# Five instructions fewer in VectorE's stream: two angle tables and pairs of column differences made in shared operations

## Chip, cores, metric

One Trainium2 chip, one core. The metric is the device time of one execution in microseconds (us). Of one execution in each job there is a profile; the span is the time from the first to the last instruction in it. Time and span differ by about 2 us, called the *time outside the span* below.

## The reference, cut

```python
xn = layernorm(x)                                   # x: [1, 2048, 512]
# A: a diagonal complex recurrence over 2048 steps
Bu = einsum("bld,pd->blp", xn + 0j, B_bar)
h_t = Lam_bar * h_{t-1} + Bu_t                      # 2048 steps, 512 complex states
yA = 2 * einsum("blp,dp->bld", hseq, C).real + xn * Dskip
# B: a gated product
yB = einsum("bsf,fd->bsd", silu(xn @ w1) * (xn @ w3), w2)   # 512 -> 1792 -> 512
out = x + yA + yB
```

The kernel works in four blocks of 512 tokens. The recurrence is turned into real scans on VectorE by rotating each state with a table of cosines and sines ("angle tables", one for each of four groups of 128 states). Part of the matrix products is done by a scheme with seven products instead of eight, which needs sums and differences of quarters of both operands (s1 to s4 of the weights, t1 to t4 of the activations, the "column differences").

## The kernel before: what the change touches

The angle table of a group is four VectorE operations, then two sines on ScalarE that are queued:

```python
def table_angles(pt):
    if pt >= 3:
        sin_step((pt - 3, 0))
    ang, rnd = slot32[pt], slot32[NPT + pt]
    nc.vector.tensor_scalar(out=ang, in0=iota_f, scalar1=turn[:, pt:pt + 1], scalar2=None, op0=ALU.mult)
    nc.vector.tensor_scalar(out=rnd, in0=ang, scalar1=MAGIC, scalar2=None, op0=ALU.add)
    nc.vector.scalar_tensor_tensor(out=ang, in0=rnd, scalar=MAGIC, in1=ang, op0=ALU.subtract, op1=ALU.subtract)
    nc.vector.tensor_scalar(out=rnd.bitcast(DT.int32), in0=ang.bitcast(DT.int32), scalar1=0x7FFFFFFF, ...)
    ...                                             # two sines appended to `sins`
```

The column differences are made for block 2 (in `bu_sums`, mixed with the weights' sums) and for block 3 (in `column_list`):

```python
((t1, b12, b11), (t2, b22, t1), (t3, b22, b12), (t4, b21, t2))   # out, x, z: out = x - z, 128x512 each
```

t1 and t3 subtract neighbours of the same kind (b12 - b11 and b22 - b12), so one operation over a wider view can make both. Small work for VectorE is queued with an estimated cost and filled in between larger steps, so a changed cost can move instructions:

```python
bg.add(1.9, lambda: table_angles(2))
bg.add(1.9, lambda: table_angles(3))
```

The first matmuls need x, normalised by VectorE, and the first columns of w1 and w3:

```python
load_w(0, 2 * P); load_w(2 * P, 4 * P)              # w1, then w3, 256 columns each time
keep_busy(NWARM, TBLK)                              # idle matmuls while nothing has landed
...
def quarter(cl, fs, parts=1):                       # chunk cl of 128 tokens
    for side, w in ((0, w1_sb), (1, w3_sb)):
        ...                                         # matmuls of 128 columns
quarter(0, (0, 1), 2)
quarter(1, (0, 1))
pps = params_transpose()                            # a tiny matmul, a useful mark in the trace
```

## Time and profile before

| | kernel before |
|---|---|
| time, median of 3 runs | 201.6 us (201.19 to 202.13) |
| profiled run: time, span | 201.48 us, 199.3 us |
| TensorE busy, VectorE busy | 195.4 us, 182.6 us |
| VectorE instructions, counted as busy / in the built program | 262 / 314 |

A busy share near 100% on TensorE says little by itself, because the ends of matmuls are modelled.

### The profile page before, as it was taken

To read this page: it belongs to the slowest core of one execution; us is meant where nothing else is said; L and a number is where in the kernel's file an instruction comes from. 1 tells how busy PE (TensorE), PEld (TensorE's weight loads), DVE (VectorE), ACT (ScalarE), POOL (GpSimd) and SP (SyncE) were. 2 spreads that over 40 slices of the span, in tenths; PEclk is the share of its full clock that TensorE was granted. 3 is DMA by queue.
4 is the path that set the end of the run, shared out by engine and by line. 5 is a ranking of instruction groups with operands and counts; after the bars stand their busy time and mean duration, and the time that the engine had idled before them with its cause. 6 is when DMAs were issued, how large, how long until landed. Compare 5 with 4: busy or idle time off the path is not lost.

```text
span 199.3 us, 3709 instructions
## 1 busy us (share of the span) xinstructions
PE 195.4 (98%) x1401; PEld 130.6 (66%) x1401; DVE 182.6 (92%) x262; ACT 134.9 (68%) x281; POOL 51.3 (26%) x75
## 2 busy tenths in 40 slices
PE   8999999999999999999999999999999999999994
PEld 2774444444444488866555478888566678888893
DVE  3699799999999999989999997999999999999972
ACT  4799897699999996968997684362588782111220
POOL 7170379800411135041202305040021303310000
PEclk9999999999999999999999999999999999999999
DMA  6999998990398054830997455838147732941111
GB/s 152 319 268 224 304 174 157 326 268 1 57 181 153 0 98 83 135 112 0 156 150 118 91 92 100 176 77 130 53 60 129 149 55 54 173 92 36 53 44 40
DMA packets 32258, 25.12 MB, mean 126 GB/s; under 512 B 16240, under 2 KB 29936, under 8 KB 32240
## 3 DMA queue, kind: packets, MB, share of 16 engines
q0 software_dynamic: 6128, 11.38, 33.6%
q1 hardware_dynamic: 25536, 13.21, 27.4%
q10 hardware_dynamic: 576, 0.30, 0.7%
q8 instruction: 11, 0.18, 0.4%
q14 instruction: 7, 0.06, 0.1%
HBM read 7.74 MB, written 2.10 MB: 49 GB/s over the span
## 4 chain that ended last, share of the span: by engine, by line
PE 95%; DMA 2%; SPq 1%; issue 0%; DVE 0%
PE gu_ps L583 34%; PE gu_ps L1043 17%; PE y_ps L1043 10%; PE gu_ps L837 7%; PE bu_ps L1043 7%; PE y_ps L450 3%; PE bu_ps L450 3%; PE y_ps L858 3%; PE y_ps L769 3%; DMA w_sb<-in_B_w_dram 2%; PE gu_ps L615 2%; PE gu_ps L769 2%; PE bu_ps L858 1%; PE bu_ps L769 1%; PE bu_ps L615 1%; SPq L166 0%
## 5 line engine op out<-in xcount | busy, mean ns | idle before, releaser
L583 PE MATMUL gu_ps<-xnT,w_sb 128*128 128x512 bf16 x312 | 69.6, 379 | 0.0
L583 PEld LDWEIGHTS <-w_sb 128*128 128x128 bf16 x312 | 30.5, 98 | 34.2
L1043 PEld LDWEIGHTS <-act 128*128 128x128 f16 x462 | 43.5, 98 | 5.4
L592 ACT ACTIVATE g<-gu_ps 128x512 bf16<-128x512 f32 x41 | 24.8, 606 | 5.9 <-PE gu_ps L583 3.1
L593 ACT ACTIVATE u<-gu_ps 128x512 bf16<-128x512 f32 x41 | 24.8, 606 | 4.4 <-PE gu_ps L583 4.1
L501 DVE TENSOR_TENSOR_SCAN u<-rho,ends,u 128x512 bf16<-128x512 f32 x16 | 20.0, 1271 | 0.0
L523 POOL DMA_DIRECT2D act<-p x7 | 9.2, 1321 | 33.9 <-DVE act L515 21.9
L1043 PE MATMUL gu_ps<-w_sb,act 128*128 128x256 bf16 (+3 forms) x126 | 15.9, 267 | 0.0
L837 PE MATMUL gu_ps<-xnT,w_sb 128*128 128x512 bf16 x64 | 15.9, 379 | 0.0
L600 DVE TENSOR_TENSOR act<-g,u 128x1024 f16<-128x1024 bf16 x21 | 14.2, 679 | 0.0
L849 ACT ACTIVATE g<-gu_ps 128x512 bf16<-128x512 f32 x14 | 8.4, 599 | 5.4 <-PE gu_ps L837 5.0
L450 PEld LDWEIGHTS <-bt 128*128 128x128 bf16 x64 | 6.3, 98 | 7.6
L1066 ACT ACTIVATE x_blk<-gu_ps 128x256 f32<-128x256 f32 (+1 forms) x9 | 3.3, 368 | 10.6 <-PE gu_ps L1043 10.6
L1043 PE MATMUL bu_ps<-w_sb,act 128*128 128x256 bf16 (+3 forms) x84 | 10.4, 264 | 0.0
L1043 PE MATMUL gu_ps<-ct,act 128*128 128x256 f16 (+1 forms) x72 | 10.4, 267 | 0.0
L837 PEld LDWEIGHTS <-w_sb 128*128 128x128 bf16 x64 | 6.2, 98 | 4.8
L501 DVE TENSOR_TENSOR_SCAN u<-rho,u 128x512 bf16<-128x512 f32 x8 | 9.2, 1207 | 0.0
L1043 PEld LDWEIGHTS <-x_blk 128*128 128x128 f16 x88 | 8.6, 98 | 1.0
L1043 PEld LDWEIGHTS <-tw 128*128 128x128 f16 x88 | 8.6, 98 | 1.0
L509 DVE TENSOR_TENSOR p<-u,tabe 128x2048 f16<-128x2048 bf16 (+1 forms) x8 | 8.7, 1085 | 0.0
L515 DVE TENSOR_TENSOR act<-u,tabe 128x2048 f16<-128x2048 bf16 (+1 forms) x8 | 8.7, 1085 | 0.0
L484 DVE TENSOR_TENSOR u<-u,tabe 128x2048 bf16<-128x2048 bf16 x7 | 8.5, 1220 | 0.1
(203 smaller groups left out, 393.9 us busy)
## 6 DMA issues: line engine op xcount, KB each, us to landing
act<-p POOLq DMA_DIRECT2D x6, 512.0 KB, 6.1
xn<-x_blk POOLq DMA_DIRECT2D x4, 512.0 KB, 6.0
out_dram<-xn SPq DMA_DIRECT2D x15, 128.0 KB, 1.7
w_sb<-in_B_w_dram SPq DMA_DIRECT2D x1, 1792.0 KB, 8.2
act<-act POOLq DMA_DIRECT2D x5, 352.0 KB, 4.6
w_sb<-in_B_w_dram SPq DMA_DIRECT2D x2, 768.0 KB, 6.1
u<-p POOLq DMA_DIRECT2D x3, 512.0 KB, 5.6
w_sb<-in_B_w_dram SPq DMA_DIRECT2D x4, 256.0 KB, 4.6
```

The costliest lines, as they stand in the source:

```text
L450: nc.tensor.matmul(out=ps, lhsT=bt[:, ri, dt, pt * P:(pt + 1) * P], rhs=xnT_blk[b][:, dt, :], start=(dt == 0), stop=(dt == NDT - 1))
L501: nc.vector.tensor_tensor_scan(out=v, data0=rho[:, pt:pt + 1].to_broadcast([P, TBLK]), data1=v, initial=init, op0=ALU.mult, op1=ALU.add)
L509: nc.vector.tensor_tensor(out=by_state(st["p16"][:, csl]), in0=by_chunk(st["g"][:, :, ::-1, tsl]), in1=by_chunk(tabe[:, psl, 2:0:-1, tsl]) ...
L515: nc.vector.tensor_tensor(out=by_state(act_state(b, hf)[:, csl]), in0=by_chunk(st["g"][:, :, :, tsl]), in1=by_chunk(tabe[:, psl, 0:1, tsl] ...
L523: gp.dma_start(out=a, in_=p16, accum_op=ALU.add)
L583: nc.tensor.matmul(out=ps[:, tsl], lhsT=w[:, dt, f * P:(f + 1) * P], rhs=xnT[:, dt, tsl], start=(dt == 0), stop=(dt == NDT - 1))
L592: nc.scalar.activation(out=g16[:, f % 2, :], in_=g_ps, func=ACT.Silu)
L593: nc.scalar.activation(out=u16[:, f % 2, :], in_=u_ps, func=ACT.Copy)
L600: nc.vector.tensor_tensor(out=act_gates(b, f - 1), in0=split(g16), in1=split(u16), op=ALU.mult)
L769: nc.tensor.matmul(out=out[:, h * TH:(h + 1) * TH], lhsT=left[:, h, k, :], rhs=right[:, k, :], start=(start and h == 0 and k == 0), stop=( ...
L837: nc.tensor.matmul(out=ps, lhsT=w[:, dt, f * P:(f + 1) * P], rhs=xnT[:, dt, :], start=(dt == 0), stop=(dt == NDT - 1))
L1043: nc.tensor.matmul(out=out, lhsT=left[:, k, :], rhs=right[k][:, cols], start=(start and k == 0), stop=(k == NK - 1), skip_group_check=True)
```

## The change

Its intent is a shorter VectorE stream: each operation has a fixed part, and a wider one pays it once (in the trace before, 128x512 took 420 ns, 128x1024 690). Tables 2 and 3 share three of their four operations (8 instructions become 5), and t1 and t3 of blocks 2 and 3 are made together (4 become 3, twice). The estimated cost of the queued sums of block 2 also goes from 0.36 to 0.38. The core of the diff:

```diff
-    def table_angles(pt):
+    def table_angles(pt, n=1):
...
-        ang, rnd = slot32[pt], slot32[NPT + pt]
-        nc.vector.tensor_scalar(out=ang, in0=iota_f, scalar1=turn[:, pt:pt + 1], ...)
+        slots = scratch[:, ...].bitcast(FP32).rearrange("p (h i t) -> p h i t", h=2, t=TBLK)
+        ang, rnd = slots[:, 0, pt:pt + n, :], slots[:, 1, pt:pt + n, :]
+        for i in range(n):
+            nc.vector.tensor_scalar(out=ang[:, i, :], in0=iota_f, scalar1=turn[:, pt + i:pt + i + 1], ...)
         nc.vector.tensor_scalar(out=rnd, in0=ang, scalar1=MAGIC, ...)          # now 128x1024, as the next two
...
-                for out, x, z in ((t1, b12, b11), (t2, b22, t1), (t3, b22, b12), (t4, b21, t2))]
+                for out, x, z in column_steps(b, t, (t1, t2, t3, t4))]
+    def column_steps(b, t, parts):
+        both = xnT_blk[b].rearrange("p (i k) (j t) -> p i k j t", i=2, j=2)
+        return ((t[:, 0::2], both[:, :, :, 1, :], both[:, 0].rearrange("p k j t -> p j k t")), (t2, b22, t1), (t4, b21, t2))
...
-    bg.add(1.9, lambda: table_angles(2))
-    bg.add(1.9, lambda: table_angles(3))
+    bg.add(3.6, lambda: table_angles(2, 2))
```

More of the change, by code (lines that the diff above doesn't have):

```diff
@@ L367, in params_w @@
         gp.tensor_scalar(out=wrn, in0=wr, scalar1=-1.0, scalar2=None, op0=ALU.mult)
-    def table_angles(pt):
-        if pt >= 3:
-            sin_step((pt - 3, 0))
-        ang, rnd = slot32[pt], slot32[NPT + pt]
-        nc.vector.tensor_scalar(out=ang, in0=iota_f, scalar1=turn[:, pt:pt + 1], scalar2=None, op0=ALU.mult)
+    def table_angles(pt, n=1):
+        if pt + n > 3:
+            sin_step((pt + n - 4, 0))
+        slots = scratch[:, 0:2 * NPT * 2 * TBLK].bitcast(FP32).rearrange("p (h i t) -> p h i t", h=2, t=TBLK)
+        ang, rnd = slots[:, 0, pt:pt + n, :], slots[:, 1, pt:pt + n, :]
+        for i in range(n):
+            nc.vector.tensor_scalar(out=ang[:, i, :], in0=iota_f, scalar1=turn[:, pt + i:pt + i + 1], scalar2=None,
+                                    op0=ALU.mult)
         nc.vector.tensor_scalar(out=rnd, in0=ang, scalar1=MAGIC, scalar2=None, op0=ALU.add)
@@ L378, in table_angles @@
                                 op0=ALU.bitwise_and)
-        for i, (src, bias, scale) in enumerate(((rnd, halfpi, -TWO_PI), (ang, 0.0, -TWO_PI))):
-            sins.append(((pt, i), lambda i=i, src=src, bias=bias, scale=scale: nc.scalar.activation(
-                out=tabe[:, pt, i, :], in_=src, func=ACT.Sin, bias=bias, scale=scale)))
+        for k in range(pt, pt + n):
+            for i, (src, bias, scale) in enumerate(((rnd, halfpi, -TWO_PI), (ang, 0.0, -TWO_PI))):
+                sins.append(((k, i), lambda k=k, i=i, src=src[:, k - pt, :], bias=bias, scale=scale: nc.scalar.activation(
+                    out=tabe[:, k, i, :], in_=src, func=ACT.Sin, bias=bias, scale=scale)))
     def weight_c(pt):
@@ L717, in column_list @@
         return [lambda out=out, x=x, z=z: nc.vector.tensor_tensor(out=out, in0=x, in1=z, op=ALU.subtract)
-                for out, x, z in ((t1, b12, b11), (t2, b22, t1), (t3, b22, b12), (t4, b21, t2))]
+                for out, x, z in column_steps(b, t, (t1, t2, t3, t4))]
+    def column_steps(b, t, parts):
+        t1, t2, t3, t4 = parts
+        b11, b12, b21, b22 = quarters(b)
+        both = xnT_blk[b].rearrange("p (i k) (j t) -> p i k j t", i=2, j=2)
+        return ((t[:, 0::2], both[:, :, :, 1, :], both[:, 0].rearrange("p k j t -> p j k t")), (t2, b22, t1), (t4, b21, t2))
     def bu_quarter(hf, kh, r, half=False):
@@ L733, in bu_columns @@
     def bu_columns(b):
-        return ups["t"] if b == 3 else [v.rearrange("p (k a) t -> p k (a t)", k=2) for v in spare_slots(k_gate(10))]
+        if b == 3:
+            return ups["t"]
+        return act(2)[:, :, k_gate(10):k_gate(10) + 4, :].rearrange("p c (k a) t -> p c k (a t)", k=2)
     def bu_sums(b):
@@ L742, in bu_sums @@
                           (s4, a12, s2, ALU.subtract)])
-        t1, t2, t3, t4 = bu_columns(b)
-        b11, b12, b21, b22 = quarters(b)
-        cols = [(*v, ALU.subtract) for v in ((t1, b12, b11), (t2, b22, t1), (t3, b22, b12), (t4, b21, t2))]
-        first = [t for two in zip(tasks[0], cols) for t in two]
-        return [(0.36, lambda out=out, x=x, y=y, op=op: nc.vector.tensor_tensor(out=out, in0=x, in1=y, op=op), ("bu", hf))
+        t = bu_columns(b)
+        cols = [(*v, ALU.subtract) for v in column_steps(b, t, [t[:, i] for i in range(4)])]
+        first = [t for two in zip(tasks[0], cols) for t in two] + tasks[0][3:]
+        return [(0.38, lambda out=out, x=x, y=y, op=op: nc.vector.tensor_tensor(out=out, in0=x, in1=y, op=op), ("bu", hf))
                 for hf, part in ((0, first), (1, tasks[1])) for out, x, y, op in part]
@@ L752, in bu_fast @@
         s1, s2, s3, s4 = bu_rows(hf)
-        t1, t2, t3, t4 = bu_columns(b)
+        t = bu_columns(b)
+        t1, t2, t3, t4 = (t[i] if b == 3 else t[:, i] for i in range(4))
         b11, b12, b21, b22 = quarters(b)
```

## The prediction

> **What bounds the kernel now.** I read the page of the kernel before first, then the chain that ended last in order of time, then TensorE's own waits, then VectorE's groups with shapes kept apart, then the timeline around the places that the change touches.
>
> The page's first part:
>
> ```profile
> PE 195.4 (98%) x1401; PEld 130.6 (66%) x1401; DVE 182.6 (92%) x262; ACT 134.9 (68%) x281; POOL 51.3 (26%) x75
> ```
>
> TensorE (PE) shows 98%, VectorE (DVE) 92%. A busy share alone does not prove that TensorE is the limit, since the ends of matmuls are modelled. So I look at the pace of their starts, in the chain that ended last (start, length, what):
>
> ```profile
> 28.41 24.17 PE gu_ps L583 x112
> 78.25 8.41 PE gu_ps L1043 x77
> 162.92 7.21 PE gu_ps L1043 x66
> ```
>
> 24.17 us over 112 matmuls of 512 columns is 215.8 ns each; 8.41 over 77 and 7.21 over 66 of 256 columns are 109.2 ns each, both times. The pace is the same early, in the middle and late. I went through the starts of all 1401 matmuls in the trace: from 8.6 us to the last one at 196.6 us, the distances are these values (and 55 to 56 ns for 128 columns) nearly without exception; what lies above them adds up to less than 0.2 us, most of it in three steps near 146, 153 and 159 us, where a matmul follows an evacuation by ScalarE (ACT) that itself follows a matmul. TensorE's own waits confirm it; this is the whole list:
>
> ```profile
> PE bu_ps L196 <- PEq L1257: 0.8, 1, 0.8
> PE gu_ps L615 <- DMA w_sb<-in_B_w_dram: 0.4, 1, 0.4
> ```
>
> Both are in the first 7 us. VectorE is waited for by TensorE's matmuls nowhere (its weight loads wait 1.0 us for a normalised x at 5 us, in code that the change leaves alone). So the time is: about 8.6 us of start, 188 us of matmuls at full pace, 2.7 us from the last matmul to the end of the span, and some 2.2 us outside the span (201.5 us for the profiled run against a span of 199.3).
>
> **What the Trainium skill says.**
> - "Perfetto Trace Analysis", section "Identifying the Most-Contended Engine": matmul occupancy is not a good measure of how near to the roofline a kernel is. I therefore rest on start distances. "TensorE: Matmul & The Clock Gate", section "Wait — 56ns, not 53.3ns?", gives 215.7 ns start to start at 512 columns once warm, and 55.6 at 128; the trace agrees (215.8 and 55 to 56 ns). There is nothing left to gain between two matmuls.
> - "VectorE: DVE Perf Modes", section "The TRN2 errata — SBUF-src ops pay a fixed extra latency per instruction": one large tile pays a fixed cost once, many small ones pay it each time; the measured fixed term is about 150 cycles. The trace agrees: with bf16 operands, one `tensor_tensor` of 512, 1024 and 2048 elements takes 420, 690 and 1219 ns, so 270 ns for 512 elements more and about 150 ns fixed. This is what the change saves.
> - Same page, section "The DRAIN you can't avoid": the next operation does not start until the pipe is empty. Here the trace says something finer, and it decides: an independent successor of a 420 ns operation starts 340 ns after its start, so before its recorded end, while one that reads its result starts 450 ns after it. So the real saving per removed instruction is about 70 to 80 ns where instructions are independent, and a merge can cost something where it puts a reader right behind its writer.
>
> **The change part by part.** The order of the instructions of the two built programs is the same on TensorE (all 2804 rows but for line numbers), on GpSimd and SyncE, and on ScalarE apart from line numbers. VectorE loses five instructions and has a few neighbours swapped. VectorE's groups before that the sums use (count, busy us, mean ns, idle before):
>
> ```profile
> L376 DVE SCALAR_TENSOR_TENSOR tw<-tw 128x512 f32<-128x512 f32 x4 | 2.8, 697 | 0.1
> L374 DVE TENSOR_SCALAR tw<-tw,turn 128x512 f32<-128x512 f32 x4 | 1.9, 478 | 1.6 <-POOL turn L325 1.6
> L377 DVE TENSOR_SCALAR tw<-tw 128x512 int32<-128x512 int32 x4 | 1.8, 442 | 0.1
> L375 DVE TENSOR_SCALAR tw<-tw 128x512 f32<-128x512 f32 x4 | 1.7, 428 | 0.1
> L966 DVE TENSOR_TENSOR tw<-ct 128x1024 f16<-128x1024 f16 x2 | 1.4, 690 | 0.0
> L717 DVE TENSOR_TENSOR x_blk<-xnT 128x512 f16<-128x512 bf16 x2 | 0.8, 418 | 0.0
> ```
>
> (1) *Angle tables 2 and 3*: 8 instructions become 5. Before: 2 x (478+428+697+442) = 4.09 us busy, and 4.08 us from start (14.79 us) to the next instruction (18.87). After, estimated: the two multiplications by a column stay (0.96); the fp32 `tensor_scalar` of 512 costs like a bf16 `tensor_tensor`, so at 1024 elements it should be about 0.70 (twice); the `scalar_tensor_tensor` runs at one element per cycle, 697 + 533 = 1.23. Sum 3.58, saving 0.51 us busy and about 0.46 us of VectorE's time. The sines of tables 2 and 3 read the result: table 2 is ready at about 18.3 us instead of 16.9, but ScalarE starts the sine of table 2 only at 25.48. No wait.
>
> (2) *Column differences for block 2* (L747): 4 instructions of 0.42 become one of 1024 elements (0.69) and two of 0.42. Start to start: 4 x 0.335 = 1.34 before, 0.60 + 2 x 0.335 = 1.27 after: 0.07 us saved. The first reader on TensorE loads weights that go with t1 at 90.28 us, 1.02 us after t1 was written; t1 now comes 0.27 us later. It still fits.
>
> (3) *The same for block 3* (L717): before, 113.51 to 114.97 = 1.46 us. After, t2 follows at once on the merged operation that it reads (0.72), t4 on t2 (0.45), then 0.34: 1.51. This one gains nothing, and may lose 0.05 us.
>
> Sum: busy time 182.6 - 0.51 - 8x0.419 + 2x0.69 + 4x0.42 = about 181.8 us in 257 instructions. Of this, TensorE sees nothing. The 0.46 us of (1) moves VectorE forward from 18.4 us; the statistics that follow are also done before a gate product that used to stand in between (0.6 us), so GpSimd's reciprocal root comes about 1 us earlier, and VectorE's wait for it (1.24 us, ending 24.57) stays a wait, merely earlier. The scans begin about 0.45 us earlier. VectorE still ends up waiting for TensorE:
>
> ```profile
> 86.77 0.69 DVE L1128 TENSOR_TENSOR xn<-gu_ps,x_blk 128x512 bf16<-128x512 f32 x1 [0.56 <-PE gu_ps L1043]
> ```
>
> There any lead from the first part is given back to idle time. The saving is hidden twice over: TensorE did not wait for VectorE, and VectorE waits for TensorE later.
>
> **The rivals.**
> - *A new wait takes the place of the old order and stalls TensorE.* The weakest place I found is near 110 us. There the copy of the states' ends (L1204) now comes ahead of a gate product (L600) that ScalarE waits for:
>
> ```profile
> 110.50 0.68 DVE L600 TENSOR_TENSOR act<-g,u 128x1024 f16<-128x1024 bf16 x1
> ...
> 111.70 0.16 DVE L1204 COPY ends<-act 128x8 f16<-128x8 f16 x1
> ```
>
>   The copy needs a transfer (act<-p, L523) issued at 104.68 and landed at 110.07. Its margin was 1.63 us and becomes about 0.4. That transfer took 5.4 us; the seven of this line took 4.2 to 8.6. If it landed x later, L600 would be x - 0.4 late, and so would ScalarE's evacuation at 111.30, which the matmul at 113.33 follows with 1.43 us to spare. So TensorE stalls only if the transfer takes more than 5.4 + 0.4 + 1.43 = 7.2 us; with the worst seen, 8.6, the loss is 1.4 us (203.0). Elsewhere (the gate products moved by 1.1 us near 35 and 52 us, and from 22.7 to about 24 us) three buffers of g and u stand between the product and its next writer; I expect no wait there.
> - *VectorE is the real bound, at 92%.* Then the saving of about 0.5 us would come through as 201.1. For it: VectorE is idle for only some us of the steady part, and ScalarE waits for L600 by 1.5 us at 111.30. Against: that ScalarE wait is absorbed before 113.5 us, and TensorE's starts show no gap there.
> - *Transfers start earlier and collide.* VectorE's lead of up to half a microsecond between 26 and 85 us moves the accumulating transfers that follow it. The mean DMA load is 126 GB/s and their readers came long after them; I give it no time.
>
> **Range and chances.** TensorE's stream is unchanged and without gaps, so I expect the median of before, 201.6 us. The three runs of before lie between 201.2 and 202.1; allowing for that spread, for 0.2 us of luck and for a rare late transfer, 201.0 to 202.3. Faster by 2% would need 4 us out of a stream that has less than 0.2 us of gaps: 1%. Slower by 2% needs several late waits at once: 1.5%.
>
> **What would show it.** Right: TensorE's two waits as before and the same pace of 215.8 and 109.2 ns; VectorE at about 181.8 us in 257 instructions; three 1024-wide instructions near 16 us of about 0.70, 1.23 and 0.70; the wait for GpSimd's root still there, ending near 23.5 us; the three instructions of block 3 no quicker than the four. Wrong: a line in TensorE's waits that names ScalarE or VectorE, a start distance above the pace near 113 us, or L1204 with idle time before it that ends with a DMA; or a span below 199 us with the same pace, which would mean that time was lost where I saw none.

## The result, and the profile after

Ratios are the mean time of one kernel's fast runs over that of the other's of the same rounds, so not quite the ratio of the medians quoted beside them.

| | before | after |
|---|---|---|
| time, median of 6 runs | 201.57 us (201.18 to 202.13) | 200.81 us (200.68 to 201.28) |
| ratio | | 0.9968, 95% interval 0.9949 to 0.9988 |
| profiled run: time, span | 201.48, 199.3 us | 200.71, 198.9 us |

The changed kernel is 0.3% quicker, well within the 2% that counts as the same, but below the predicted range of 201.0 to 202.3 us.

The page of the kernel after, first part:

```profile
PE 195.2 (98%) x1401; PEld 130.7 (66%) x1401; DVE 182.2 (92%) x257; ACT 135.0 (68%) x281; POOL 50.9 (26%) x75
```

The chain that ended last, after (start, length, what; the three pieces that answer to those of before):

```profile
27.98 24.17 PE gu_ps L587 x112
77.83 8.41 PE gu_ps L1055 x77
162.49 7.21 PE gu_ps L1055 x66
```

The lengths are the same to the last digit. All that differs is where the pieces stand: 0.43, 0.42 and 0.43 us earlier. So TensorE's pace did not change, and what it gained in this run it had already gained by 28 us. The timeline of TensorE around 7 us shows where; its last line is the transpose of the parameters, the mark. First before, then after (start, length, operation, in brackets the idle time and what ended it):

```profile
6.11 0.61 PE L615 MATMUL gu_ps<-xnT,w_sb 128*128 128x128 bf16 x8
7.12 1.35 PE L615 MATMUL gu_ps<-xnT,w_sb 128*128 128x128 bf16 x21 [0.40 <-DMA w_sb<-in_B_w_dram]
...
8.56 0.18 PE L315 MATMUL y_ps<-ident,par_rows 12*128 12x12 bf16 x1
```

```profile
6.16 2.04 PE L619 MATMUL gu_ps<-xnT,w_sb 128*128 128x128 bf16 x32
8.14 0.18 PE L315 MATMUL y_ps<-ident,par_rows 12*128 12x12 bf16 x1
```

Before, the ninth of these matmuls waited for the first columns of w3, which landed at 7.07 us in this execution; after, they landed at 6.64. The first merged instruction stands at 15.30 us, eight microseconds later: no merged work comes early enough to have brought that load in. TensorE's waits after, the whole list:

```profile
PE bu_ps L196 <- PEq L1268: 0.8, 1, 0.8
PE y_ps L243 <- DVE xn L224: 0.2, 1, 0.2
```

So two of the prediction's own signs of being wrong came up: a line that names VectorE (0.2 us, for the first normalised x, in code that the change leaves alone), and a span below 199 us at the same pace. Both lie in the start.

The lengths of the merged instructions are as worked out. VectorE's groups by shape, after (count, busy us, mean ns, idle before):

```profile
L379 DVE SCALAR_TENSOR_TENSOR tw<-tw 128x1024 f32<-128x1024 f32 x1 | 1.2, 1224 | 0.0
L380 DVE TENSOR_SCALAR tw<-tw 128x1024 int32<-128x1024 int32 x1 | 0.7, 695 | 0.0
L378 DVE TENSOR_SCALAR tw<-tw 128x1024 f32<-128x1024 f32 x1 | 0.7, 694 | 0.0
L721 DVE TENSOR_TENSOR x_blk<-xnT 128x1024 f16<-128x1024 bf16 x1 | 0.7, 685 | 0.0
```

The stretch of tables 2 and 3 saved more than was worked out. Its first line and the line that follows it, before and then after:

```profile
14.79 0.48 DVE L374 TENSOR_SCALAR tw<-tw,turn 128x512 f32<-128x512 f32 x1
18.87 0.69 DVE L219 BATCH_NORM_STATS2 stats<-x_blk 128x6 f32<-128x512 bf16 x1
```

```profile
14.39 0.88 DVE L376 TENSOR_SCALAR tw<-tw,turn 128x512 f32<-128x512 f32 x2
17.90 0.69 DVE L219 BATCH_NORM_STATS2 stats<-x_blk 128x6 f32<-128x512 bf16 x1
```

From 4.08 us it fell to 3.51, so VectorE gained 0.57 us here and not 0.46: the two multiplications now stand side by side and together take 0.88 us in place of 0.96, which is most of the difference. None of it reached TensorE's pace.

And the tight place near 110 us. Block 3's first difference and the line that follows the four, before:

```profile
113.51 0.42 DVE L717 TENSOR_TENSOR x_blk<-xnT 128x512 f16<-128x512 bf16 x1
114.97 0.69 DVE L600 TENSOR_TENSOR act<-g,u 128x1024 f16<-128x1024 bf16 x1
```

VectorE's timeline there after:

```profile
110.01 0.17 DVE L1215 COPY ends<-act 128x8 f16<-128x8 f16 x1
110.08 0.69 DVE L604 TENSOR_TENSOR act<-g,u 128x1024 f16<-128x1024 bf16 x1
...
113.01 0.69 DVE L721 TENSOR_TENSOR x_blk<-xnT 128x1024 f16<-128x1024 bf16 x1
113.73 0.88 DVE L721 TENSOR_TENSOR x_blk<-xnT,x_blk 128x512 f16<-128x512 bf16 x2
114.53 0.68 DVE L604 TENSOR_TENSOR act<-g,u 128x1024 f16<-128x1024 bf16 x1
```

The copy of the ends shows no idle time: its transfer had landed at 109.58, 0.43 us ahead. Block 3's differences take 113.01 to 114.53 = 1.52 us, against 1.46 before.

There is a second piece. Time minus span is 2.18 us for the profiled run before and 1.81 after; over the six runs after it is 1.74 to 1.88. The prediction took this time as given.

### The profile page after: what moved, and what is told of

Read it like the earlier page. It is cut to its first block, busy times and chain, and to the rows that moved or that the text cites. A ratio compares the mean times of both kernels' runs of the same rounds, so it can differ in the third digit from the quotient of the medians.

```text
span 198.9 us, 3703 instructions
## 1 busy us (share of the span) xinstructions
PE 195.2 (98%) x1401; PEld 130.7 (66%) x1401; DVE 182.2 (92%) x257; ACT 135.0 (68%) x281; POOL 50.9 (26%) x75
## 4 chain that ended last, share of the span: by engine, by line
PE 96%; DMA 1%; DVE 1%; issue 0%
PE gu_ps L587 34%; PE gu_ps L1055 18%; PE y_ps L1055 10%; PE gu_ps L849 7%; PE bu_ps L1055 7%; PE y_ps L454 3%; PE bu_ps L454 3%; PE y_ps L870 3%; PE y_ps L781 3%; PE gu_ps L619 2%; PE gu_ps L781 2%; PE bu_ps L781 1%; PE bu_ps L870 1%; DMA x_blk<-in_A_x_dram 1%; PE bu_ps L619 1%; PE y_ps L243 1%
```

## The experiments

For every timed run the span is listed to 0.1 us, so the time outside of a single run is good to 0.05 us, and each table below splits the mean time in span and time outside. "Kernel before, same job" is the kernel before, run in the same rounds on the same chip.

### First job: repeats, and each part alone

`e1_before_again` is the kernel before with one comment line added, `e2_after_again` the changed kernel with one comment line added. There is no other edit. `e3_tables_only` takes from the change the tables alone:

```diff
-    def table_angles(pt):
+    def table_angles(pt, n=1):                      # and its body, as in the change
-    bg.add(1.9, lambda: table_angles(2))
-    bg.add(1.9, lambda: table_angles(3))
+    bg.add(3.6, lambda: table_angles(2, 2))
```

and `e4_columns_only` takes the rest:

```diff
-                for out, x, z in ((t1, b12, b11), (t2, b22, t1), (t3, b22, b12), (t4, b21, t2))]
+                for out, x, z in column_steps(b, t, (t1, t2, t3, t4))]      # and the same in bu_sums
```

Expected (the letters A to E name rival explanations, each defined where it first stands):

> The kernel before, unchanged but for a comment: how much two copies of one program differ here. Theory A (the 0.3% is variation of the start: the landing of the first weights near 7 us and the time outside the span, neither touched by the change): ratio to before within 0.9975 to 1.0025, and single runs scattered over 201.1 to 202.2 us, with spans that differ by 0.4 us from run to run. Theory B (the gain is VectorE's shorter stream): ratio 1.000, scatter as before, which alone tells nothing.

> The changed kernel, unchanged but for a comment. Theory A in its pure form (chance): the ratio goes back towards 1, 0.998 to 1.001, and the spans mix 198.9 and 199.4 as often as the kernel before does. Theory B (a real effect of the change): the ratio stays at 0.996 to 0.998. Theory C (something that goes with the built program and not with VectorE's work, such as where its code and buffers lie, shifts the start): also 0.996 to 0.998, but the spans' difference sits before 8 us in the profile, and TensorE's pace after that is the same.

> Only the angle tables are merged (three instructions less, near 16 us). Theory B: this is the larger part of VectorE's saving (0.46 us), so at least two thirds of the gain: ratio about 0.998. Theory A: 1.000 within 0.0015. Theory C: anything from 0.996 to 1.002, not in proportion to the instructions removed. In every theory: TensorE's pace after 8 us unchanged, three 1024-wide instructions of about 0.69, 1.22 and 0.70 us.

> Only the column differences are merged (two instructions less, near 89 and 113 us). Theory B: VectorE's time is the same within 0.1 us, so ratio 1.000. Theory A: 1.000 within 0.0015. Theory C: anything from 0.996 to 1.002. The angle tables are as before, and the start up to 14 us is the same sequence as in all others.

Measured:

| run | VectorE instructions in the program | runs | mean span (least to most) | mean outside | ratio, 95% interval |
|---|---|---|---|---|---|
| kernel before, same job | 314 | 11 | 199.30 (198.8 to 199.7) | 2.16 | |
| e1_before_again | 314 | 6 | 199.27 (198.9 to 199.5) | 2.19 | 0.9998, 0.9983 to 1.0013 |
| e2_after_again | 309 | 6 | 199.37 (198.8 to 199.8) | 1.79 | 0.9983, 0.9966 to 1.0001 |
| e3_tables_only | 311 | 6 | 199.42 (199.0 to 199.7) | 1.81 | 0.9991, 0.9977 to 1.0004 |
| e4_columns_only | 312 | 6 | 199.15 (198.7 to 199.9) | 2.03 | 0.9985, 0.9966 to 1.0003 |

The ratios alone decide nothing: they overlap. The split does. The spans of all five differ by less than their own scatter of about 0.3 us from run to run, and the changed kernel's is even 0.07 us longer here than that of the kernel before. The time outside the span is another matter: each kernel's values lie within 0.12 us of its mean, and the changed kernel's largest (1.81) is far below the smallest of the kernel before (2.09). Theory B, that VectorE's shorter work comes through, has no support: nothing of it is in the span. The pure form of theory A, all chance, falls too, because 0.37 us outside the span is not chance. Theory C, something that goes with the program and not with VectorE's work, has the right kind of cause but placed it before 8 us, inside the span.

The spans' scatter has its origin at the start, as far as it was profiled. In thirteen profiles (before, after, and all runs but e8, which adds work) the time from the mark at about 8 us, the transpose of the parameters, to the end of the last matmul is 188.03 or 188.04 us. The mark itself stands anywhere from 7.93 (e4) to 8.79 us (e10). Two of TensorE's lists of waits show that what holds the start varies even with the same program; first e1 (the same program as the kernel before), then e4:

```profile
PE bu_ps L196 <- PEq L1257: 0.8, 1, 0.8
PE y_ps L243 <- DVE xn L224: 0.7, 1, 0.7
```

```profile
PE bu_ps L196 <- PEq L1265: 0.8, 1, 0.8
```

In e1 TensorE waits 0.7 us for the first normalised x, where the kernel before, the same program, waited for w3; in e4 neither wait is on the list.

### Second job: the number of instructions, the start, and VectorE's slack

`e5_after_plus5` adds to the changed kernel, and `e6_before_plus5` to the kernel before, five tiny writes to a tile that nothing reads, at a time when VectorE waits for x:

```diff
     nc.gpsimd.memset(mhalf, -0.5)
+    idle = const.tile([P, 5], FP32, name="idle")
+    for i in range(5):
+        nc.vector.memset(idle[:, i:i + 1], 0.0)
```

`e7_start_order` changes the order of the first matmuls of the changed kernel:

```diff
-            quarter(0, (0, 1), 2)
-            quarter(1, (0, 1))
+            quarter(0, (0, 1), 2, (0,))             # w1, chunk 0
+            quarter(1, (0, 1), 1, (0,))             # w1, chunk 1
+            quarter(0, (0, 1), 2, (1,))             # w3, chunk 0
+            quarter(1, (0, 1), 1, (1,))             # w3, chunk 1
```

`e8_vector_plus2` gives VectorE idle work in the kernel before, behind the angle tables:

```diff
+    def burn():
+        spare = scratch[:, 9 * 2 * TBLK:11 * 2 * TBLK].bitcast(BF16).rearrange("p (a t) -> p a t", a=4)
+        for _ in range(2):
+            nc.vector.tensor_tensor(out=spare, in0=w1_sb[:, :, 0:TBLK], in1=w1_sb[:, :, 0:TBLK], op=ALU.mult)
+    bg.add(0.0, burn)
```

Expected:

> The changed kernel with five one-column memsets added to VectorE's stream in the first microsecond, when it waits for x: as many VectorE instructions as before (314 in the built program), all the merged operations kept. So far the spans of all kernels are alike (means 199.2 to 199.4 us) but the time outside the span is 2.17 us in the kernel before, 2.03 with the columns merged, 1.81 with the tables merged, 1.79 with both. Theory D (the number of instructions in VectorE's stream sets that outside time, whatever they do): outside time back to 2.1 to 2.3 us, ratio to before 0.999 to 1.001. Theory E (the merged operations themselves matter): outside time stays at 1.75 to 1.85, ratio about 0.998.

> The kernel before with the same five memsets (319 VectorE instructions). Theory D with a steady slope of some 0.07 us each: outside time about 2.5 us, ratio 1.0015 to 1.002. Theory D with a threshold (crossed between 314 and 309): outside time stays at 2.1 to 2.25, ratio 1.000 within 0.0015. Theory E: 2.17 as well, so only e5 tells E from D. In all: spans as before, since VectorE is idle there.

> The changed kernel with another order of the first matmuls: all those with w1 for the first two chunks, then those with w3, so that the late landing of the first part of w3 (6.4 to 7.1 us) is met later. Theory A (spread of the span comes from that landing alone, since from the transpose of the parameters to the last matmul every run so far took 188.03 us): the spread of the spans shrinks, the transpose of the parameters starts near 8.25 us in every run, no wait for w3 at the ninth such matmul; mean time within 0.2 us of the changed kernel. If the spread stays at 1 us, something else at the start varies too.

> The kernel before with two idle products of 128x2048 (1.13 us of VectorE's time each, start to start) behind the angle tables near 18.9 us: five times the saving of the tables, in the other direction. Prediction's view (TensorE bound, VectorE's margin at the tightest place before 85 us is 0.5 us, at the weight load of 75.58 us that follows the sum act<-act,x_blk): the first 0.6 us of the 2.27 vanish, TensorE waits 1.4 to 1.8 us near 75 us, time 202.9 to 203.4 us, ratio 1.007 to 1.009. If VectorE were the bound: +2.3 us, ratio 1.011. If VectorE had free slack throughout: ratio 1.000.

Measured:

| run | VectorE instructions in the program | runs | mean span (least to most) | mean outside | ratio, 95% interval |
|---|---|---|---|---|---|
| kernel before, same job | 314 | 11 | 199.32 (198.9 to 199.6) | 2.16 | |
| e5_after_plus5 | 314 | 6 | 199.20 (198.8 to 199.7) | 2.16 | 0.9994, 0.9979 to 1.0009 |
| e6_before_plus5 | 319 | 5 | 199.22 (199.1 to 199.4) | 2.16 | 0.9995, 0.9983 to 1.0007 |
| e7_start_order | 309 | 5 | 199.38 (199.1 to 199.6) | 1.78 | 0.9984, 0.9972 to 0.9996 |
| e8_vector_plus2 | 317 | 4 | 201.18 (201.1 to 201.3) | 1.98 | 1.0082, 1.0067 to 1.0096 |

**e5 settles what the steady part of the gain is.** It does all the merged work of the changed kernel, and its five added instructions run where VectorE has nothing to do. Its timeline at the start:

```profile
0.79 0.17 DVE L212 MEMSET idle<- 128x1 f32 x5 [0.79 <-PEq L1271]
3.18 0.69 DVE L222 BATCH_NORM_STATS2 stats<-x_blk 128x6 f32<-128x512 bf16 x1 [2.22 <-DMA x_blk<-in_A_x_dram]
```

They take 0.17 us, and 2.22 us of idle time follow. Yet the time outside goes back from 1.79 to 2.16 us, to the kernel before's value. Theory E, that the merged operations themselves matter, is out; the number of instructions, not the work, moves this time. e6 says that there is no steady slope: 319 is like 314.

**e7** did what it was built for: the ninth such matmul waits for ScalarE's copy of chunk 1 instead of w3, and the mark stands at 8.28 us in its profile.

```profile
6.00 0.61 PE L620 MATMUL gu_ps<-xnT,w_sb 128*128 128x128 bf16 x8
6.84 1.50 PE L620 MATMUL gu_ps<-xnT,w_sb 128*128 128x128 bf16 x24 [0.24 <-ACT xnT L244]
8.28 0.18 PE L315 MATMUL y_ps<-ident,par_rows 12*128 12x12 bf16 x1
```

But its spans still scatter, from 199.1 to 199.6 with a deviation of 0.19 us over five runs, like the 0.20 of the kernel before in the same job. So the landing of w3 is one source of the start's scatter, and not the only one, as e1 had shown with x. The order gains nothing and was not kept.

**e8** tests the argument that the whole prediction stands on: VectorE 92% busy, and not the bound, but with small margins. The products took 2.39 us of VectorE's stream (18.70 to 21.09 us in the trace), and the time rose by 1.7 us (mean 203.15 against 201.48), within the range expected. But by the split above this is a sum of two things: the span rose by 1.86 us, and the time outside fell by 0.18. The first three of TensorE's waits in e8:

```profile
PE bu_ps L1043 <- DVE act L1085: 1.2, 1, 1.2
PE bu_ps L196 <- PEq L1264: 0.8, 1, 0.8
PE gu_ps L583 <- ACT g L592: 0.4, 1, 0.4
```

The first is the place that was named, the sum in front of the weight load (75.58 us before, 77.46 here); there the starts lie 1.32 us further apart than the pace, a little less than the 1.4 to 1.8 expected. The third was not named: at 45 us ScalarE waited 1.44 us for a gate product of VectorE, and TensorE for ScalarE; there the starts lie 0.59 us further apart than the pace. So 1.91 of the 2.39 us came through, in two places and not one, and the total met its range partly by luck. VectorE's slack over the first half is real but only about 0.5 us; the saving of the change runs the other way, and there a margin only grows.

### Third job: is it VectorE's count, and exactly?

The same block of memsets, with five on GpSimd (`nc.gpsimd.memset`, e9) or three or two on VectorE (`range(3)`, e10; `range(2)`, e11), in the changed kernel; with two on VectorE in the kernel before (e12). The diff is that of e5 with another engine or number.

> The changed kernel with the five one-column memsets on GpSimd instead of VectorE (VectorE 309 instructions as in the changed kernel, GpSimd 127 instead of 122). Theory D, narrow (VectorE's count alone sets the time outside the span): outside time 1.75 to 1.85 us. If any five instructions more bring the lost time back: 2.1 to 2.2. Spans as before either way.

> The changed kernel with three idle VectorE memsets: 312 instructions, as many as with only the columns merged, where the outside time was 2.03 us. Theory D: 1.98 to 2.08 us here as well. If the work that was merged matters instead: 1.75 to 1.85.

> The changed kernel with two idle VectorE memsets: 311 instructions, as many as with only the tables merged, where the outside time was 1.81 us. Theory D: 1.76 to 1.86 us. A steady slope through 1.80 at 309 and 2.16 at 314 would give 1.95 instead.

> The kernel before with two idle VectorE memsets: 316 instructions, between 314 (2.16 us outside) and 319 (2.16), next to the 317 of the kernel with two wide idle products, which had 1.98. Theory D with a plateau from 314 on: 2.1 to 2.2, and then the 1.98 of that other kernel came from its later end and not from its count. Theory D without plateau: 1.95 to 2.0.

Measured:

| run | VectorE instructions in the program | runs | mean span (least to most) | mean outside (least to most) | ratio, 95% interval |
|---|---|---|---|---|---|
| kernel before, same job | 314 | 11 | 199.29 (198.8 to 199.8) | 2.18 (2.10 to 2.24) | |
| e9_after_plus5_gpsimd | 309 | 6 | 199.10 (198.8 to 199.4) | 1.78 (1.74 to 1.81) | 0.9971, 0.9957 to 0.9986 |
| e10_after_plus3 | 312 | 6 | 199.33 (198.8 to 199.9) | 2.03 (1.99 to 2.10) | 0.9995, 0.9975 to 1.0016 |
| e11_after_plus2 | 311 | 6 | 199.28 (198.9 to 199.7) | 1.81 (1.74 to 1.88) | 0.9984, 0.9968 to 1.0001 |
| e12_before_plus2 | 316 | 6 | 199.38 (198.9 to 200.2) | 1.86 (1.83 to 1.90) | 0.9989, 0.9969 to 1.0009 |

Programs with different work and the same VectorE count have the same time outside the span: at 312, 2.03 with only the columns merged (e4) and 2.03 with everything merged and three idle memsets (e10); at 311, 1.81 twice (e3, e11); at 314, 2.16 to 2.19 for the kernel before in four groups and 2.16 for e5; at 309, 1.78 to 1.81 in four groups, one of them with five more instructions on GpSimd (e9). Three of the four expectations came in on the number. One more count differs: the page's total falls by six, 3709 to 3703, because TensorE's sequencer executes one semaphore wait less wherever the columns are merged (10 in place of 11; the prediction had found TensorE's rows of the built programs the same). It plays no part here: e3 has 11 and e11 10, and both have 1.81.

e12 missed both of its ranges. With 316 instructions the time outside is 1.86, lower than at 314 and at 319. So the curve goes 1.79 (309), 1.81 (311), 2.03 (312), 2.16 (314), 1.86 (316), 1.98 (317), 2.16 (319): up, down and up again. More instructions are not worse as such. The 1.98 of e8 scatters more than the others (1.87 to 2.15 in four runs), and no other kernel has 317, so whether its count or its later end makes it is open.

What in the launch or the end of a program depends on that count, and whether it lies before the first instruction or after the last, none of these runs shows: the time is outside what the profile covers. An obvious candidate is the fetch of instructions in blocks, which could give a rising and falling curve. But the pages count its packets on two queues, and all fourteen show the same 11 (16 KB each) and 7 (8 KB), so no run fetched a block more or less within the span. This candidate has no support, though nothing excludes it. The cause of the curve stays open.

## Why the prediction was wrong

**What held.** From the mark on, TensorE's stream was unchanged and without gaps, no new wait appeared on it, and VectorE's saving did not reach it. The 1024-wide instructions took 0.694, 1.224 and 0.695 us, against estimates of 0.70, 1.23 and 0.70. Block 2 saved 0.07 us as worked out, and block 3 lost 0.06 us (estimated 0.05), for the reason given: t2 follows on the merged operation that it reads. The margin at the copy of the ends became 0.43 us ("about 0.4"). The wait for GpSimd's root stayed, and ended at 23.26 us (about 23.5 was foreseen; this run's start was 0.4 us earlier). The rival of VectorE as the real bound, with 201.1 us, would have come nearer to the measured 200.81, but for a wrong reason: e5 keeps the shorter work, and the gain is gone.

**What failed.** The step is the first one, where the prediction put the time together from its parts: "about 8.6 us of start, 188 us of matmuls at full pace, 2.7 us from the last matmul to the end of the span, and some 2.2 us outside the span". The 188 and the 2.7 stood (188.03 and 2.77 us in the changed kernel's profile). The other two were carried over as constants.

- *2.2 us outside the span* became 1.80. This is the steady part of the gain: 2.17 (mean of the kernel before's runs in three jobs and e1) to about 1.79, some 0.38 us or 0.2%, with VectorE's count and not with its work, as e5, e10 and e11 show.
- *8.6 us of start* is one draw: the mark stood at 8.56 us in the profile of before and lies between 7.93 and 8.79 over the thirteen profiles. In the first comparison the changed kernel had a good draw, which is luck. The six runs of before average 201.54 us; less 2.17 outside, that is a span of 199.37. The changed kernel's six average 199.10. Of the difference of 0.63 us, 0.36 is outside the span and 0.27 is start. When the changed kernel was run again (e2), its mean span was 199.37, 0.07 more than the kernel before beside it, and the ratio 0.9983 in place of 0.9968.

Both were needed for the miss. The steady part alone takes the mean of before from 201.54 to about 201.16 us, still above the lower end of the range, 201.0; e2's mean is 201.15. The lucky start did the rest.

The range was too narrow for both: three runs of before do not show how a span scatters by up to 1 us, and a time outside the profile was taken as none of the change's business.

**A smaller slip.** VectorE's busy time came to 182.2 us, not 181.8. The prediction had itself found that independent instructions start 0.34 us apart though each lasts 0.42, so their busy times overlap; but in the sum of busy times it subtracted the full 0.42 for each. With start-to-start differences for the columns (0.07 saved in block 2, 0.06 lost in block 3), and for the tables the difference of their busy times without overlaps in the traces, 3.97 less 3.49, the sum is 182.6 - 0.48 - 0.07 + 0.06 = 182.1. The prediction's 0.46 us of VectorE's own time for the tables was 0.57, mostly for the same reason: the two multiplications are independent and overlap, and it gave each its full length.

## What to carry to other kernels

When the engine that sets the pace has no gaps, look for a small change's effect where the trace does not look: subtract the span from the time of every run before explaining a few tenths of a microsecond, and repeat the unchanged kernel to see how its start scatters. To tell work from count, put back the instructions without the work: idle writes in a place where the engine waits. And merge operations for the bound engine or a tight margin; on an engine with slack the merge buys margin, not time.

## What the Trainium skill lacked or had wrong

- "Runtime: NRT & Kernel Launch", section "The ~15µs preamble/postamble breakdown", lists stages before and after the kernel with a time each, "depending on engine count and DMA setup". It names no dependence on the number of instructions of an engine. Here the time outside the span went with VectorE's count: 1.79 us at 309, 2.03 at 312, 2.17 at 314, 1.86 at 316, 2.16 at 319; five more instructions on GpSimd left it at 1.78, and the counts of ScalarE and SyncE were not varied. No run shows which of the listed stages, if any, the 2 us belong to.
- "VectorE: DVE Perf Modes", section "The DRAIN you can't avoid": the next operation does not start until the pipe is empty, but one "that is not held starts earlier". So the page is not wrong here; it gives no time for this. The runs show independent successors starting 0.34 us after the start of an operation of 0.42 us (before its recorded end), and readers of its result 0.45 us after it.
- Same page, section "The perf-mode tier table (the rule you actually need)", has no row for `scalar_tensor_tensor`. In fp32 it took 697 ns at 512 elements and 1224 at 1024, so 1.03 ns for each further element, where `tensor_scalar` in fp32 took 428 and 694, 0.52 ns.
